# Attention coefficients spread by DMA through DRAM instead of by TensorE, with a new order of first loads, a last tile in two halves and sorted final waits

## The chip, the cores and the metric

The kernel runs on one core of one Trainium2 chip. The metric is device time in microseconds (us) of one execution. Times of single instructions come from one profiled execution of the kernel, taken by the hardware profiler; its own time stands beside the median of the unprofiled runs in the table below.

## The reference

The kernel computes two layers, each made of a linear attention with a learned feature map (A) and a gated feed-forward (B), with residuals around both. The weights are the same in both layers. There are 2048 tokens of width 512, 32 heads of 16, and a hidden width of 1376.

```python
def _A_ref(x, wqkv, w_phi, wo):          # D = 512, H = 32, Dh = 16
    q, k, v = split_heads(x @ wqkv)
    pq = einsum("bhsd,hdf->bhsf", q, w_phi)
    pk = einsum("bhsd,hdf->bhsf", k, w_phi)
    phi_q = concat([softmax(pq), softmax(-pq)], -1)
    phi_k = concat([softmax(pk), softmax(-pk)], -1)
    kv = einsum("bhsf,bhsd->bhfd", phi_k, v)
    z = einsum("bhsf->bhf", phi_k)
    o = einsum("bhqf,bhfd->bhqd", phi_q, kv) / (einsum("bhqf,bhf->bhq", phi_q, z)[..., None] + 1e-6)
    return merge_heads(o) @ wo

def _B_ref(x, W_gate, W_up, W_down):
    return (relu(x @ W_gate) * (x @ W_up)) @ W_down

for layer in range(2):
    x = x + _A_ref(layernorm(x), wqkv, w_phi, wo)
    x = x + _B_ref(layernorm(x), W_gate, W_up, W_down)
```

All tensors are bf16. The kernel folds w_phi into the query and key weights once, at the start (`fold`, giving `Wqp` and `Wkp`).

## The kernel before, in words

**Tiles and slabs.** The 2048 tokens are 16 tiles of 128 tokens (one per partition), and four slabs of four tiles. The code counts slabs from 0 (`st`); the text counts them from 1, so slab 1 is `st` 0. The whole activation stays in SBUF (`x_sb`); DRAM is touched by the loads at the start and by one output DMA for each tile at the end.

**Steps of a slab.** `into_a(st)` makes the layernorm and `keys`: the matmuls of keys and values for each tile, the two exponentials (`expk`, line 484, ScalarE), their sums (`Zk`, VectorE), and `vhat`, the values divided by the sums (line 495, GpSimd), from which TensorE adds up `kvsum`. `sums()` runs once in a layer, after all four slabs: it spreads `kvsum` into the block-diagonal weights `kvbd` and `ZDw`. `out_of_a(st)` makes `queries` (matmuls with `Wqp`, exponentials into `expq`), `attend` and the second layernorm. `glu(st)` makes the feed-forward: 11 chunks of hidden width, each with four matmuls into a gate bank and four into an up bank, ReLU on ScalarE (line 612), the product on VectorE (line 614), then 11 matmuls with `Wd` for each of the four tiles, and the residual (line 597).

**attend.** For each token and head there are two coefficients (one for each sign of the feature map), which divide the unnormalised exponentials by their sums and by the denominator. They are worked out with tokens in the partitions (`atok`, line 561), and TensorE transposes them to `aT`: 64 rows (2 signs x 32 heads) of 512 tokens. `expq` has heads times features in its partitions: eight groups (four chunks `c` by two signs `sg`) of 128 rows, each row set of 16 belonging to one head. So each of 64 rows must be repeated 16 times. The kernel does this by a matmul with the 0/1 matrix `EC`: eight matmuls of 512 columns for a slab, each into a PSUM bank (line 570). For sign 0 VectorE multiplies `expq` by the bank (line 578); for sign 1 (`VIA`) ScalarE first copies the bank to SBUF (`absb`, line 574) and VectorE multiplies by that copy (line 575). Two matmuls with `kvbd` for each chunk then make the numerator (`num`), ScalarE copies it to `oT` (line 583), and four matmuls for each tile with `wo_sb` make the projection. In slab 1 the residual is added by a fifth matmul and copied by ScalarE (line 592), in the others VectorE adds it (line 597).

**The order of the work.** Nothing in the order is written by hand. Every operation is put down with its readers and writers, a cost (`occ`, `lat`) and, for a DMA, a number of bytes; `Program.schedule` then goes through them as a list scheduler: at each step it takes the ready operation with the earliest possible start, and among equal starts the one that was put down first. `plan` sorts by start, gives every engine its fixed instruction order, and works out which semaphores must be waited for. A DMA is priced at 560 ns on its issuing engine, then 630 ns, then its bytes at 270 bytes per ns on one shared queue, then 1170 ns. Every DMA takes the next of 60 semaphores in turn (`N_DSEM`), and at the end `emit` has SyncE (SP) wait for each semaphore that was used, by its number. Loops in the source order are: all four `into_a`, then in each layer `sums`, `out_of_a(0)`, and for each slab `out_of_a(st + 1)`, `glu(st)`, and `into_a(st)` for the next layer or the output DMAs.

**First loads.** On SP: the first tile of x, `wphi`, the second tile of x, `wv`, the rest of x, and the remaining weights. On ScalarE's queue: the key weights in two halves (`ld wk`), ahead of the activation table load.

**Buffers that the change touches.** `expk` and `vhat` have six buffers each (`NE`), `hT` nineteen (`NH`), `absb` three (`NA`).

## Time and profile before

| | |
|---|---|
| Median of 3 runs | 426.74 us (426.41 to 426.89) |
| Profiled execution, its own time | 427.2 us |
| Span of the profiled execution | 425.5 us |
| TensorE (PE) busy | 416.8 us, 98% of the span, 2576 matmuls |
| VectorE (DVE) busy | 278.7 us, 66% |
| ScalarE (ACT) busy | 226.1 us, 53% |
| GpSimd (POOL) busy | 69.2 us, 16% |
| DMA | 10.95 MB in 9598 packets, mean 26 GB/s |

The span runs from the first instruction to the last; the execution's own time has about 1.7 us around it. In the page and the trace's answers, a group of instructions is shown by line, engine, operation and tiles, with busy time and mean duration, and the idle time of the engine before it with what ended that. All matmuls have line 322 (the helper `mm`) and all transposes line 326, so they are told apart by their tiles: `pb<-aT,EC` are the spreading matmuls of `attend`. A matmul's recorded duration is that of a pipelined instruction; the distance from start to start is what it occupies. The page's first part has the busy time of each engine, its second part the span in 40 slices of 10.6 us: VectorE is busy in tenths `7989768984589548883775446887536734863332` of them.

### The profile page before, as it was taken

The numbers are of one execution on the slowest core, as the hardware profiler recorded it, in microseconds if no ns is written. First come the engines' busy times: TensorE is split into PE (matmuls) and PEld (weight loads), VectorE is DVE, ScalarE is ACT, GpSimd is POOL, SyncE is SP. The second block draws the span as 40 slices with busy tenths as digits, with TensorE's granted clock in tenths as the row PEclk, the third lists the DMA queues.
The fourth block names the chain that finished last, engine by engine and source line by source line (L and its number), as shares of the span: only waits on it lengthen the run. The fifth ranks groups of instructions, "written<-read, shape, count | busy, mean of one in ns | idle before, by whom it ended". The sixth has DMA issues, their size and how long they took to land.

```text
span 425.5 us, 6563 instructions
## 1 busy us (share of the span) xinstructions
PE 416.8 (98%) x2576; PEld 209.9 (49%) x2576; DVE 278.7 (66%) x582; ACT 226.1 (53%) x460; POOL 69.2 (16%) x71
## 2 busy tenths in 40 slices
PE   7899999999999999999999999999999999999997
PEld 3455555445445545454455445645444444454443
DVE  7989768984589548883775446887536734863332
ACT  6999888955084514742182169894514522550320
POOL 0439680000008000620043007000000000000000
DMA  8940000000000000000000000000000001000001
GB/s 270 383 144 2 2 0 2 2 1 2 1 2 1 2 0 2 0 2 0 2 0 2 1 2 1 2 2 0 2 25 27 1 0 51 0 2 34 17 0 49
DMA packets 9598, 10.95 MB, mean 26 GB/s; under 512 B 1024, under 2 KB 8544, under 8 KB 9568
## 3 DMA queue, kind: packets, MB, share of 16 engines
q1 hardware_dynamic: 9024, 10.01, 7.0%
q10 hardware_dynamic: 544, 0.52, 0.4%
q8 instruction: 20, 0.33, 0.3%
q14 instruction: 10, 0.08, 0.1%
HBM read 8.44 MB, written 2.10 MB: 25 GB/s over the span
## 4 chain that ended last, share of the span: by engine, by line
PE 88%; ACT 9%; DMA 1%; DVE 0%; SPq 0%; POOL 0%; issue 0%
PE pb L322 85%; PE pb L326 3%; ACT expk L484 3%; ACT ytile L446 2%; DMA wv<-in_A_wqkv_dram 1%; ACT vsb L492 1%; ACT expq L536 1%; ACT Wqp L417 0%; ACT hT L406 0%; ACT yT L460 0%; POOL vhat L495 0%; SPq L345 0%; ACT lnv L435 0%; DVE x_sb L597 0%; DVE atok L561 0%
## 5 line engine op out<-in xcount | busy, mean ns | idle before, releaser
L612 ACT ACTIVATE gate_sb<-pb 128x512 bf16<-128x512 f32 (+1 forms) x88 | 52.7, 598 | 123.3 <-PE pb L322 123.2
L495 POOL TENSOR_TENSOR vhat<-vsb,rZk 128x544 bf16<-128x544 bf16 x64 | 68.4, 1104 | 195.3 <-DVE rZk L488 181.5
L614 DVE TENSOR_TENSOR hT<-gate_sb,pb 128x512 bf16<-128x512 bf16 (+1 forms) x88 | 59.7, 682 | 59.9 <-PE pb L322 59.3
L322 PE MATMUL pb<-yT,Wu 128*128 128x512 bf16 (+1 forms) x352 | 92.8, 379 | 0.0
L322 PE MATMUL pb<-yT,Wg 128*128 128x512 bf16 (+1 forms) x352 | 92.6, 379 | 0.0
L322 PE MATMUL pb<-Wd,hT 128*128 128x512 bf16 (+1 forms) x352 | 77.4, 379 | 0.0
L597 DVE TENSOR_TENSOR x_sb<-x_sb,pb 128x512 bf16<-128x512 bf16 x56 | 36.9, 685 | 46.8 <-PE pb L322 46.7
L322 PEld LDWEIGHTS pb<-Wd,hT 128*128 128x128 bf16 (+1 forms) x352 | 34.4, 98 | 41.5
L322 PEld LDWEIGHTS pb<-yT,Wu 128*128 128x128 bf16 (+1 forms) x352 | 35.1, 100 | 38.5
L322 PEld LDWEIGHTS pb<-yT,Wg 128*128 128x128 bf16 (+1 forms) x352 | 34.6, 100 | 36.8
L486 DVE TENSOR_REDUCE Zk<-expk 128x64 f32<-128x1024 bf16 x32 | 38.4, 1202 | 13.4 <-ACT expk L484 13.3
L432 DVE BATCH_NORM_STATS2 stats<-x_sb 128x6 f32<-128x512 bf16 x64 | 42.5, 676 | 1.9 <-DMA x_sb<-in_A_x_dram 1.1
L536 ACT ACTIVATE expq<-pb 128x512 bf16<-128x512 f32 x64 | 35.3, 703 | 12.8 <-PE pb L322 12.8
L484 ACT ACTIVATE expk<-pb 128x512 bf16<-128x512 f32 x64 | 37.0, 667 | 4.6 <-PE pb L322 3.4
L322 PE MATMUL pb<-wv,yT 128*128 128x512 bf16 x128 | 33.8, 379 | 1.3 <-DMA wv<-in_A_wqkv_dram 1.3
L322 PE MATMUL pb<-wo_sb,oT 128*128 128x512 bf16 x128 | 34.9, 379 | 0.0
L322 PE MATMUL pb<-Wkp,yT 128*128 128x512 bf16 x128 | 33.4, 379 | 1.1 <-ACT yT L460 1.1
L322 PE MATMUL pb<-yT,Wqp 128*128 128x512 bf16 x128 | 32.4, 379 | 0.6 <-ACT Wqp L417 0.5
L574 ACT ACTIVATE absb<-pb 128x512 bf16<-128x512 f32 x32 | 17.8, 623 | 21.3 <-PE pb L322 21.0
L460 ACT ACTIVATE yT<-pb 128x512 bf16<-128x512 bf16 x52 | 27.4, 607 | 2.8 <-PE pb L326 2.7
L322 PE MATMUL pb<-vhat,expk 128*128 128x136 bf16 x256 | 24.3, 223 | 0.1
L322 PEld LDWEIGHTS pb<-vhat,expk 128*128 128x128 bf16 x256 | 18.5, 98 | 10.4 <-POOL vhat L495 1.3
(66 smaller groups left out, 384.5 us busy)
## 6 DMA issues: line engine op xcount, KB each, us to landing
out_dram<-x_sb SPq DMA_DIRECT2D x16, 128.0 KB, 1.7
x_sb<-in_A_x_dram SPq DMA_DIRECT2D x3, 512.0 KB, 9.2
Wg<-in_B_W_gate_dram SPq DMA_DIRECT2D x1, 1376.0 KB, 10.6
Wu<-in_B_W_up_dram SPq DMA_DIRECT2D x1, 1376.0 KB, 12.9
Wd<-in_B_W_down_dram SPq DMA_DIRECT2D x1, 1280.0 KB, 15.8
hT<-in_A_wqkv_dram ACTq DMA_DIRECT2D x2, 256.0 KB, 3.5
wv<-in_A_wqkv_dram SPq DMA_DIRECT2D x1, 512.0 KB, 6.0
hT<-in_A_wqkv_dram SPq DMA_DIRECT2D x1, 512.0 KB, 8.3
```

The costliest lines, as they stand in the source:

```text
L322: op("pe", lambda e: e.matmul(view(ps), lhsT, rhs, start=start, stop=stop), reads=reads, writes=[ps], occ=max(25.0, 0.4167 * n + 2.6), lat ...
L326: op("pe", lambda e: e.transpose(view(ps), src, ident[:]), reads=list(reads) + [R("ident")], writes=[ps], occ=56, lat=220, name=name)
L432: op("dve", (lambda t: lambda e: e.bn_stats(stats[:, t, :], x_sb[:, t, :]))(t), reads=[R("x", t)], writes=[R("st", t)], occ=580, lat=680, ...
L460: op("act", (lambda ps, dst: lambda e: e.activation(dst, b16half(ps).rearrange("p (c n) -> p c n", c=NC), ACT.Copy))(ps, dst), reads=[ps], ...
L484: op("act", (lambda i, s, pk: lambda e: e.activation(expk[:, i, s, :], full(pk), ACT.Exp, scale=1.0 - 2.0 * s))(i, s, pk), reads=[pk], wri ...
L486: op("dve", (lambda i, zb: lambda e: e.tensor_reduce(Zk[:, zb, :], expk[:, i, :, :].rearrange("p s (h f) -> p (s h) f", f=16), AX.X, ALU.a ...
L495: op("pool", (lambda i, s, vb, rz: lambda e: e.tensor_tensor(vhat[:, i, s, :, :], vsb[:, vb, :, :], rZk[:, rz, s * 32:(s + 1) * 32].unsque ...
L536: op("act", (lambda c, s, ps: lambda e: e.activation(expq[:, st, c, s, :], full(ps), ACT.Exp, scale=1.0 - 2.0 * s))(c, s, ps), reads=[ps], ...
L574: op("act", (lambda ab, ps: lambda e: e.activation(absb[:, ab, :], full(ps), ACT.Copy))(ab, ps), reads=[ps], writes=[R("absb", ab)], occ=4 ...
L597: op("dve", lambda e: e.tensor_tensor(x_sb[:, t, :], x_sb[:, t, :], full(ps), ALU.add), reads=[R("x", t), ps], writes=[R("x", t)], occ=597 ...
L612: op("act", (lambda m, gb, pg: lambda e: e.activation(gate_sb[0:m, gb, :], pg.f32()[0:m, :], ACT.Relu))(m, gb, pg), reads=[pg], writes=[R( ...
L614: op("dve", (lambda m, gb, hb, pu: lambda e: e.tensor_tensor(hT[0:m, hb, :], gate_sb[0:m, gb, :], pu.f32()[0:m, :], ALU.mult))(m, gb, hb, pu),
```

## The change

- In slabs 2 to 4 of both layers, `attend` makes no `EC` matmuls. SP stores `aT` (64 rows, 64 KB) to a DRAM tensor (two of them, in turn), waits for that DMA, and issues eight loads; each reads eight rows 16 times over and fills one 128 x 512 tile of `abT` in SBUF. VectorE multiplies `expq` by these tiles. Slab 1 keeps its matmuls, and its ScalarE copies go to `abT`. The columns of `atok` are put in the order of the eight groups.
- `abT` has eight tiles, one for each group, and is shared by all slabs; `absb` goes. `expk` and `vhat` have five buffers instead of six, `hT` eighteen instead of nineteen.
- `wphi` is loaded first on ScalarE's queue, ahead of the key weights, and is priced at 131072 bytes; on SP the second tile of x follows the first.
- The last tile of the last layer is computed in two halves of 256 columns, each with its own eleven matmuls, residual and output DMA; the first half's DMA is issued by ScalarE, the second's by SP.
- At the end SP waits for the DMA semaphores in the order of their last use.

```diff
--- before.py
+++ after.py
@@ -195,6 +195,7 @@
         count = {s: 0 for s in streams}
         known = {e: {s: 0 for s in streams} for e in ENGINES}
         past = {s: {0: {t: 0 for t in streams}} for s in streams}
+        self.last = {}
         self.waits, self.seq = {}, {e: [] for e in ENGINES}
         rr = 0
         for o in order:
@@ -204,6 +205,7 @@
                 assert x.cnt is not None, (o.name, x.name)
                 need[x.stream] = max(need.get(x.stream, 0), x.cnt)
             if o.is_dma:
+                self.last[rr % N_DSEM] = rr
                 o.stream = rr % N_DSEM
                 rr += 1
                 if count[o.stream]:
@@ -239,9 +241,8 @@
             else:
                 ins.then_inc(sems[e], 1)
         if e == "sp":
-            for s in range(N_DSEM):
-                if self.count[s]:
-                    eng.wait_ge(dsems[s], 16 * self.count[s])
+            for s in sorted((s for s in range(N_DSEM) if self.count[s]), key=lambda s: self.last[s]):
+                eng.wait_ge(dsems[s], 16 * self.count[s])
 
 
 def build_kernel(nc, A_x, A_wqkv, A_w_phi, A_wo, W_gate, W_up, W_down, out):
@@ -262,7 +263,7 @@
             return E(nc.sbuf_tensor(name, [P] + list(shape), dt))
 
         NWARM = 8
-        NY, NYT, NE, NV, NG, NH, NA = 4, 6, 6, 4, 3, 19, 3
+        NY, NYT, NE, NV, NG, NH = 4, 6, 5, 4, 3, 18
         x_sb = sb("x_sb", [NT, 512])
         ytile = sb("ytile", [NY, 512])
         yT = sb("yT", [NYT, NC, 512])
@@ -302,7 +303,8 @@
         ident = sb("ident", [128])
         mask8a = sb("mask8a", [8])
         mask8 = sb("mask8", [8])
-        absb = sb("absb", [NA, 512])
+        abT = sb("abT", [8, 512])
+        scratch = [nc.dram_tensor(f"spread{i}", (64, 512), BF16, kind="Internal").ap() for i in range(2)]
         pb = [E(nc.psum_tensor(f"pb{i}", [P, 512], FP32)) for i in range(8)]
 
         made = {}
@@ -346,12 +348,12 @@
                 writes=[R("x", t) for t in range(t0, t1)], nbytes=(t1 - t0) * 131072, name=f"ld x{t0}")
 
         load_x(0, 1)
+        load_x(1, 2)
+        dma("act", lambda e: e.dma_start(wphi[:], A_w_phi.rearrange("(kc hl) d f -> (hl d) kc f", hl=8)),
+            writes=[R("wphi")], nbytes=131072, name="ld wphi")
         for c in (0, 2):
             dma("act", (lambda c: lambda e: e.dma_start(Wknat[:, c:c + 2, :], wqkv_v[:, c:c + 2, 512:1024]))(c),
                 writes=R_Wnat["k"][c:c + 2], nbytes=262144, name="ld wk")
-        dma("sp", lambda e: e.dma_start(wphi[:], A_w_phi.rearrange("(kc hl) d f -> (hl d) kc f", hl=8)),
-            writes=[R("wphi")], nbytes=65536, name="ld wphi")
-        load_x(1, 2)
         dma("sp", lambda e: e.dma_start(wv[:], wqkv_v[:, :, 1024:1536]), writes=[R("wv")], nbytes=524288, name="ld wv")
         load_x(2, 4)
         load_x(4, 8)
@@ -419,8 +421,8 @@
 
         fold("k", Wknat, Wkp)
 
-        cnt = {"y": 0, "yT": 0, "e": 0, "h": 0, "g": 0, "v": 0, "a": 0}
-        VIA = lambda st, c, sg: sg == 1
+        cnt = {"y": 0, "yT": 0, "e": 0, "h": 0, "g": 0, "v": 0, "s": 0}
+        VIA = lambda c, sg: sg == 1
 
         def layernorm(st, step=4, early=False):
 
@@ -558,25 +560,35 @@
             op("act", lambda e: e.activation(zr[:, g], zden[:, g], ACT.Ln), reads=[R("zden", g), R("tables")], writes=[R("zr", g)], occ=200, lat=300, name="zln")
             op("act", lambda e: e.activation(zr[:, g], zr[:, g], ACT.Exp, scale=-1.0), reads=[R("zr", g)], writes=[R("zr", g)], occ=200, lat=300, name="zr")
             for s in range(2):
-                op("dve", (lambda s: lambda e: e.tensor_tensor(atok[:, g, :, s * 32:(s + 1) * 32], Zs[:, g, :, 1 - s, :], zr[:, g], ALU.mult))(s),
+                op("dve", (lambda s: lambda e: e.tensor_tensor(atok[:, g, :, 0:64].rearrange("p t (c s h) -> p t c s h", s=2, h=8)[:, :, :, s, :], Zs[:, g, :, 1 - s, :].rearrange("p t (c h) -> p t c h", h=8),
+                                                               zr[:, g].rearrange("p t (c h) -> p t c h", h=8), ALU.mult))(s),
                    reads=[R("Zs", g), R("zr", g)], writes=[R("atok", g)], occ=195, lat=290, name="atok")
             pa = bank(f"aT{st}")
             for tt in range(4):
                 tr(pa, (lambda tt: lambda p: p.b16()[:, tt * 128:(tt + 1) * 128])(tt), atok[:, g, tt, :], [R("atok", g)], f"aTt{st}")
             op("dve", lambda e: e.tensor_copy(aT[:, g, :], b16half(pa)), reads=[pa], writes=[R("aT", g)], occ=328, lat=415, name="aT")
+            if st:
+                scr = scratch[cnt["s"] % 2]
+                cnt["s"] += 1
+                rs = R("scr", cnt["s"] % 2)
+                dma("sp", lambda e: e.dma_start(scr, aT[0:64, g, :]), reads=[R("aT", g)], writes=[rs], nbytes=65536, name=f"aTo{st}")
+                for gi in range(8):
+                    dma("sp", (lambda gi: lambda e: e.dma_start(abT[:, gi, :], scr[8 * gi:8 * gi + 8, :].unsqueeze(1).to_broadcast([8, 16, 512])))(gi),
+                        reads=[rs], writes=[R("abT", gi)], nbytes=260000, name=f"abT{st}")
             for c in range(NC):
                 for sg in range(2):
-                    ps = bank(f"ab{st}{c}{sg}")
-                    mm(ps, full, EC[:, sg * 4 + c, :], aT[:, g, :], True, True, [R("EC"), R("aT", g)], 512, f"ab{st}")
-                    if VIA(st, c, sg):
-                        ab = cnt["a"] % NA
-                        cnt["a"] += 1
-                        op("act", (lambda ab, ps: lambda e: e.activation(absb[:, ab, :], full(ps), ACT.Copy))(ab, ps), reads=[ps], writes=[R("absb", ab)], occ=480, lat=610, name=f"abc{st}")
-                        op("dve", (lambda c, sg, ab: lambda e: e.tensor_tensor(expq[:, st, c, sg, :], expq[:, st, c, sg, :], absb[:, ab, :], ALU.mult))(c, sg, ab),
-                           reads=[R("eq", st, c, sg), R("absb", ab)], writes=[R("eq", st, c, sg)], occ=335, lat=420, name=f"em{st}", port=True)
-                    else:
+                    gi = 2 * c + sg
+                    if st == 0:
+                        ps = bank(f"ab{st}{c}{sg}")
+                        mm(ps, full, EC[:, gi, :], aT[:, g, :], True, True, [R("EC"), R("aT", g)], 512, f"ab{st}")
+                    if st == 0 and not VIA(c, sg):
                         op("dve", (lambda c, sg, ps: lambda e: e.tensor_tensor(expq[:, st, c, sg, :], expq[:, st, c, sg, :], full(ps), ALU.mult))(c, sg, ps),
-                           reads=[R("eq", st, c, sg), ps], writes=[R("eq", st, c, sg)], occ=595, lat=690, name=f"em{st}")
+                           reads=[R("eq", st, c, sg), ps], writes=[R("eq", st, c, sg)], occ=597, lat=690, name=f"em{st}")
+                        continue
+                    if st == 0:
+                        op("act", (lambda gi, ps: lambda e: e.activation(abT[:, gi, :], full(ps), ACT.Copy))(gi, ps), reads=[ps], writes=[R("abT", gi)], occ=480, lat=610, name=f"abc{st}")
+                    op("dve", (lambda c, sg, gi: lambda e: e.tensor_tensor(expq[:, st, c, sg, :], expq[:, st, c, sg, :], abT[:, gi, :], ALU.mult))(c, sg, gi),
+                       reads=[R("eq", st, c, sg), R("abT", gi)], writes=[R("eq", st, c, sg)], occ=335, lat=425, name=f"em{st}", port=True)
                 pn = bank(f"num{st}{c}")
                 for sg in range(2):
                     mm(pn, full, kvbd[:, sg, c, :], expq[:, st, c, sg, :], sg == 0, sg == 1, [R("kvbd", sg, c), R("eq", st, c, sg)], 512, f"num{st}")
@@ -596,7 +608,7 @@
         def residual(t, ps):
             op("dve", lambda e: e.tensor_tensor(x_sb[:, t, :], x_sb[:, t, :], full(ps), ALU.add), reads=[R("x", t), ps], writes=[R("x", t)], occ=597, lat=690, name=f"res{t}")
 
-        def glu(st, b):
+        def glu(st, b, last=False):
             slots = []
             for fc in range(NF):
                 m = 128 if fc < NF - 1 else FL
@@ -615,12 +627,20 @@
                    reads=[R("gate", gb), pu], writes=[R("hT", hb)], occ=597, lat=690, name=f"h{st}")
             for tt in range(4):
                 t = 4 * st + tt
-                ps = bank(f"d{t}")
-                for fc, hb in enumerate(slots):
-                    m = 128 if fc < NF - 1 else FL
-                    mm(ps, full, hT[0:m, hb, tt * 128:(tt + 1) * 128], Wd[0:m, fc, :], fc == 0, fc == NF - 1,
-                       [R("hT", hb), R("Wd") if fc < NF - 1 else R("WdL")], 512, f"d{t}")
-                residual(t, ps)
+                halves = ((0, 256), (256, 512)) if last and t == NT - 1 else ((0, 512),)
+                for n0, n1 in halves:
+                    ps = bank(f"d{t}")
+                    for fc, hb in enumerate(slots):
+                        m = 128 if fc < NF - 1 else FL
+                        mm(ps, (lambda n: lambda p: p.f32()[:, 0:n])(n1 - n0), hT[0:m, hb, tt * 128:(tt + 1) * 128], Wd[0:m, fc, n0:n1], fc == 0, fc == NF - 1,
+                           [R("hT", hb), R("Wd") if fc < NF - 1 else R("WdL")], n1 - n0, f"d{t}")
+                    if n1 - n0 == 512:
+                        residual(t, ps)
+                    else:
+                        op("dve", (lambda t, n0, n1, ps: lambda e: e.tensor_tensor(x_sb[:, t, n0:n1], x_sb[:, t, n0:n1], ps.f32()[:, 0:n1 - n0], ALU.add))(t, n0, n1, ps),
+                           reads=[R("x", t), ps], writes=[R("xe", n0)], occ=330, lat=420, name=f"res{t}")
+                        dma("sp" if n0 else "act", (lambda t, n0, n1: lambda e: e.dma_start(outv[:, t, n0:n1], x_sb[:, t, n0:n1]))(t, n0, n1),
+                            reads=[R("xe", n0)], writes=[R("out", n0)], nbytes=65536, name=f"out{t}")
 
 
         outv = out.rearrange("b (t p) d -> p (b t) d", p=P)
@@ -644,12 +664,12 @@
             b0 = out_of_a(0)
             for st in range(NS):
                 b1 = out_of_a(st + 1) if st + 1 < NS else None
-                glu(st, b0)
+                glu(st, b0, layer == 1)
                 b0 = b1
                 if layer == 0:
                     into_a(st)
                 else:
-                    for t in range(4 * st, 4 * st + 4):
+                    for t in range(4 * st, min(4 * st + 4, NT - 1)):
                         dma("sp", (lambda t: lambda e: e.dma_start(outv[:, t, :], x_sb[:, t, :]))(t), reads=[R("x", t)], writes=[R("out")], nbytes=131072, name=f"out{t}")
 
         prog.schedule()
```

## The prediction

> **What bounds the kernel now.** I read the chain that ended last, then TensorE's rows in order of time, then the windows by stage.
>
> ```profile
> PE 88%; ACT 9%; DMA 1%; DVE 0%; SPq 0%; POOL 0%; issue 0%
> L322 PE MATMUL pb<-aT,EC 128*128 128x512 bf16 x64 | 17.3, 381 | 0.0
> 88.78 1.03 PE L322 MATMUL pb<-yT,Wu 128*128 128x512 bf16 x4
> 89.64 1.03 PE L322 MATMUL pb<-yT,Wg 128*128 128x512 bf16 x4
> 90.50 1.03 PE L322 MATMUL pb<-yT,Wu 128*128 128x512 bf16 x4
> ```
>
> The chain is TensorE from about 48 to 422.6 us and ScalarE (9%) from 10 to 47. Four matmuls of 512 columns start 0.86 us after the four before them, so one occupies TensorE for 0.2157 us (the 379 ns of a record is a pipelined span, not a price). Nothing is idle between them: what leaves TensorE here leaves the end, if nothing else comes late.
>
> ```profile
> core 0: us, PE busy (x) PEld busy (x) DVE busy (x) ACT busy (x) POOL busy (x), PEclk, DMA share, GB/s
> 71.00:87.00 16.00, 16.00 (x115) 8.04 (x115) 13.81 (x37) 14.96 (x33) 0.00 (x0) 1.00 0.01 2
> 87.00:250.00 163.00, 163.00 (x903) 80.96 (x901) 109.91 (x205) 68.74 (x139) 25.56 (x24) 1.00 0.00 1
> 274.00:291.00 17.00, 16.96 (x121) 8.16 (x120) 13.56 (x37) 15.72 (x34) 0.00 (x0) 1.00 0.00 1
> ```
>
> The windows give busy time by engine. From 87 on VectorE has a third free, ScalarE more, DMA is empty. The two starts of a layer (71 to 87, 274 to 291) are different: all three engines are nearly full, because slab 1's attention and layernorm must be over before the first GLU matmul (87.05 us).
>
> **The matmuls that go.** Six attends (slabs 2 to 4, two layers) lose eight EC matmuls each: 48 x 0.2157 = 10.35 us. VectorE gains too: 24 products move from PSUM to SBUF sources, 676 to 415 ns, 24 x 0.26 = 6.3 us, and ScalarE drops 24 copies (623 ns records, about 0.5 us apart). Neither counts by itself, off the chain.
>
> ```profile
> L578 DVE TENSOR_TENSOR expq<-expq,pb 128x512 bf16<-128x512 bf16 x32 | 21.3, 676 | 0.7 <-PE pb L322 0.7
> L575 DVE TENSOR_TENSOR expq<-expq,absb 128x512 bf16<-128x512 bf16 x32 | 13.0, 415 | 0.0
> L574 ACT ACTIVATE absb<-pb 128x512 bf16<-128x512 f32 x32 | 17.8, 623 | 21.3 <-PE pb L322 21.0 <-DVE mv L433 0.3
> ```
>
> **What replaces them.** One store of aT to DRAM, a wait for it on SP, and eight spreading loads, nine DMAs on SP's queue.
>
> ```profile
> out_dram<-x_sb SPq DMA_DIRECT2D x16, 128.0 KB, 1.7
> 2.26 0.43 SPq L355 DMA_DIRECT2D wv<-in_A_wqkv_dram  x1
> 2.73 1.02 SPq L345 DMA_DIRECT2D x_sb<-in_A_x_dram  x2
> 3.15 0.69 DVE L432 BATCH_NORM_STATS2 stats<-x_sb 128x6 f32<-128x512 bf16 x1 [0.35 <-DMA x_sb<-in_A_x_dram]
> ```
>
> The store costs at most the 1.7 us of an output tile of twice its size. A 128 KB load takes 2.3 us (x's first tile was issued at 0.80, its reader started at 3.15). So the first coefficients are there 1.7 + 0.05 + 2.3 = 4.1 us after the store's issue. Loads follow each other by SP's issue, 0.43 to 0.51 us: the last is there after 7.3 us. No row shows a DMA that reads each row 16 times. From below, the page's peak of 383 GB/s would move 128 KB in 0.34 us, under the issue; from above, SP's issue of 1.42 us for Wg into full queues would make the last 14.0 us. I take about 0.8 us a load, the last after 9.7 us: nearer the short rows, since the queues are empty, with an allowance for the repeated reading. The planner prices a load at 260000 / 270 = 0.96 us and its first at 4.9 us, the last at 11.7, so in the written order VectorE should find coefficients landed when it reaches a product.
>
> The Trainium skill, "DMA: Bandwidth & Descriptors", section "Rules for kernel authors", speaks against these loads: an outermost dimension under 16, here the eight heads, keeps a DMA on at most that many of the 16 engines. No row of before has such a DMA. An estimate by the rule: queue q1's 7.0% of 16 engines' span for 9024 packets is 53 ns a packet, so 128 packets on eight engines take 0.85 us a load and the last lands after 10.0 us instead of 7.3; the sum would be the same for slabs 3 and 4.
>
> What hides those 10 us: for slabs 3 and 4 the GLU of an earlier slab, 132 matmuls or 28.5 us, which TensorE can take first; slab 4 of layer 2 also needs products, projection, residual and layernorm (some 10 us) and still fits. Without that cover 10 us would be paid each time. The loads also stand on SP ahead of output DMAs in layer 2, but these come 2.4 us apart four at a time (first at 314.8 us), and only the last matters.
>
> **Slab 2, at the start of a layer**, has no GLU to hide behind. There its eight EC matmuls were fillers:
>
> ```profile
> 80.43 0.38 PE L322 MATMUL pb<-aT,EC 128*128 128x512 bf16 x1
> 80.86 1.03 PE L322 MATMUL pb<-aT,EC 128*128 128x512 bf16 x4
> 87.05 0.81 PE L322 MATMUL pb<-yT,Wg 128*128 128x512 bf16 x3
> 87.70 1.03 PE L322 MATMUL pb<-wo_sb,oT 128*128 128x512 bf16 x4
> ```
>
> aT of slab 2 is copied at 71.2; its coefficients then land between 75.7 and 81.5. Of slab 1's chain, three products of slab 2 leave VectorE (11 products from 71.55 to 76.8 where slab 1 needs 8: 1.3 us) and three matmuls leave TensorE (0.65 us), so the GLU can start 1 to 1.7 us earlier; num and wo of slab 2 fill from about 78. Bounds: at best the small stalls there now (about 0.5 us a start) vanish as well, -0.5; at worst GLU starts at 85.3 with all 16 wo matmuls of slab 2 left (3.45 us) where now it starts at 87.05 with 4 left (0.86): 88.75 against 87.91 is 0.84 later where 1.73 earlier was counted, +2.6. I take +0.7 a start, 1.4 us in all, near the low end because TensorE has num, wo, transposes and slab 3's and 4's zd matmuls in reach.
>
> **One buffer fewer for expk and vhat** (six to five), and 18 instead of 19 for hT. The tenth tile's exponentials ran at 40.17 us; with five buffers they wait for slab 2's kv matmuls, whose last ten start at 40.89 and end by 41.5. That is up to 1.3 us on ScalarE in the stage it bounds; other applies and copies can be put in front, so 0.3, bounds 0 and 1.3. For hT, eleven of 18 slots belong to one GLU and the next needs its eighth after its first 28 matmul pairs: 0.
>
> **Head.** wphi leaves SP, so x's second tile and wv are issued about 0.47 us earlier; it goes first on ScalarE's queue, so both wk loads, the table load and EC come 0.47 us later. The first exponentials start at 9.91 and need both wv (landed 8.28) and Wkp (copied by 8.24): one comes earlier, one later. Bounds -0.4 and +0.6; I take +0.2, since wk now also meets wv in the queues.
>
> **Tail.** The residual of half a tile: by the rows 571 ns for 408 columns and 429 for 272, 412 ns for 256, against 685: -0.27; 22 matmuls of 256 columns for 11 of 512: +0.03. The final waits:
>
> ```profile
> L244 SPq EVENT_SEMAPHORE  x16: 17/28/28, 423.7 to 425.0; - x16
> SPq L244 <- DMA out_dram<-x_sb: 0.4, 1, 0.4
> ```
>
> 32 DMAs are waited for in 16 records, the first at 423.7; without the 0.4 us spent on the last DMA they run 0.06 us apart and end at 424.6. The change has 16 loads, 54 spreading DMAs and 17 output DMAs, 87 on 60 semaphores: 60 waits, 30 records, 1.8 us from 0.4 us after the last issue, so 2.2 where the landing now ends it at 1.7: +0.45. Putting them in the order of use can't shorten a row of waits already met; it only keeps the last DMA last. Bounds: -0.2 if waits cost nothing and 64 KB lands sooner, +0.5. Tail together -0.27 + 0.03 + 0.45 = +0.2, between -0.5 and +0.3.
>
> **The sum**, for the profiled execution of 427.2 us (span 425.5, 1.7 around it): 427.2 - 10.35 + 1.4 (starts) + 0.3 (expk) + 0.2 (head) + 0.2 (tail) = 418.95. The median of 426.74 lies 0.46 lower: 418.5.
>
> **Rivals.** First, TensorE's saving is paid in full: the DMA is empty and VectorE and ScalarE are relieved at the starts as well, which speaks for it; against it, TensorE needs something to do in those 16 us. 426.74 - 10.35 - 0.5 (stalls) + 0.2 = 416.1. Second, slab 2's coefficients are exposed at both starts: for it speaks that DVE and ACT are at 86% and 93% there, against it that wo can run before the last product. 2 x 2.6 for 2 x 0.7: 418.5 + 3.8 = 422.3. Third, and slower: the spreading loads are slower than the planner's 0.96 us, so VectorE, which runs in its written order, stands before a product with the GLU's hT products (L614) queued behind it, and TensorE stops when its eight PSUM banks are full. The real first landing leads the plan by 0.8 us, and TensorE can run ahead by about 2 us (two or three free banks, each filled in 0.86 us); the saving left is 8.2 / 6 = 1.4 us a slab. So it decides from 0.8 + 2 + 1.4 = 4.2 us over seven loads, that is 0.96 + 0.6 = 1.6 us a load; at 2.0 us a load the lag is 7 x 1.04 - 0.8 = 6.5, less 2, times 6 = 27 us, less 8.2: 445. Against it stand all load rows of this trace, 1.4 us for as much as 512 KB at the page's 383 GB/s. Fourth, the spreading leaves TensorE but the end is set elsewhere, and nothing changes: VectorE's third of free time speaks against it.
>
> **How the numbers follow.** 0.5 for the forecast, 0.24 for the full saving, 0.17 for slab 2 exposed, 0.07 for late loads, 0.02 for no change. A difference under 0.2% (0.85 us) can't be told from none. Faster 0.91, same 0.02, slower 0.07. The range takes in the first two rivals with their unknowns (416.1 less 0.4 for the head; 422.3 and 0.7 of the expk bound): 415.7 to 423.0; the last two, 0.09, and some of the edges lie outside.
>
> **What would show it.** Right: 16 matmuls aT,EC are left; TensorE's busy time falls by about 10 us and stays without gaps from the GLU of slab 1 on; between the last wo of slab 1 and that GLU there are gaps of about a microsecond in each layer; the products of slabs 2 to 4 take 415 ns and idle little before them; loads land 4 to 10 us after the store's issue; 30 records of final waits end about 2.2 us after the last issue. Wrong: VectorE's products waiting for abT by microseconds in slabs 3 and 4 with hT products behind them (third rival), or gaps of over 2 us before the first GLU matmul (second), or first exponentials well after 9.9 us (head).

## The result, and the profile after

The changed kernel takes 422.14 us (median of 4 runs, 421.48 to 423.47), beside 426.81 us (4 runs, 426.41 to 427.12) of the kernel before on the same chip: a ratio of 0.9895, 95% interval 0.9869 to 0.9921, or 4.5 us less where 8.3 us less was forecast. The time lies inside the predicted range and the sign is right, but nearly half of the expected gain is missing. The profiled execution took 421.89 us, its span is 420.2.

The page of the changed kernel: TensorE's row of part 1, the engines' shares of the chain from part 4, and from part 5 the products with coefficients out of SBUF.

```profile
PE 410.0 (98%) x2539; PEld 207.5 (49%) x2539; DVE 272.7 (65%) x583; ACT 214.9 (51%) x436; POOL 69.0 (16%) x71
PE 83%; DVE 7%; ACT 4%; DMA 3%; POOL 1%; issue 1%; SPq 0%; ACTq 0%
L590 DVE TENSOR_TENSOR expq<-expq,abT 128x512 bf16<-128x512 bf16 x56 | 21.9, 418 | 5.7 <-DMA abT<-spread 5.6
```

TensorE still carries the chain, but VectorE has 7% of it (0% before) and DMA 3% (1%): something new stands in TensorE's way. The products take 418 ns as forecast, and the idle time before them is small, 5.7 us over 56. TensorE's busy time fell by 6.8 us, not by the 10.35 that its matmuls occupied: a record of 379 ns is longer than the 216 ns that a matmul occupies, so a matmul that starts 0.1 us late still looks busy. Lateness is therefore measured here from start to start, against the median distance of a matmul's kind (traces of other kernels lack some 2% of the matmul records; such a hole of 0.22 us is not counted). By it the matmuls from the first spreading matmul of layer 1 on were 1.4 us late in all before and are 5.3 us late now, and 10.35 - 3.9 is about the 6.8.

The windows by stage of the changed kernel, with the columns of those shown of before; the last row is the six microseconds in which slab 2's loads run.

```profile
core 0: us, PE busy (x) PEld busy (x) DVE busy (x) ACT busy (x) POOL busy (x), PEclk, DMA share, GB/s
72.00:88.00 16.00, 15.37 (x110) 7.34 (x108) 13.30 (x38) 13.40 (x30) 0.00 (x0) 1.00 0.23 75
272.00:288.00 16.00, 15.45 (x113) 7.62 (x114) 13.35 (x39) 14.17 (x32) 0.00 (x0) 1.00 0.24 79
76.00:82.00 6.00, 6.00 (x52) 3.10 (x53) 4.36 (x14) 5.00 (x11) 0.00 (x0) 1.00 0.51 175
```

TensorE is idle 0.63 and 0.55 us in the two starts, where it was idle 0.00 and 0.04. While the loads run, the 16 DMA engines are busy 0.51 of the time: half of them work. At 175 GB/s a load of 131 KB takes 0.75 us.

The timeline of the changed kernel at the start of layer 1: SP's queue, then VectorE, then TensorE (start, duration, in brackets the idle time before and who ended it).

```profile
72.51 0.53 SPq L574 DMA_DIRECT2D spread<-aT  x1
74.52 5.05 SPq L576 DMA_DIRECT2D abT<-spread  x8
```

```profile
77.32 0.43 DVE L590 TENSOR_TENSOR expq<-expq,abT 128x512 bf16<-128x512 bf16 x1 [0.90 <-DMA abT<-spread]
```

```profile
84.26 0.38 PE L324 MATMUL pb<-expq,kvbd 128*128 128x512 bf16 x1 [0.34 <-DVE ytile L451]
88.31 1.04 PE L324 MATMUL pb<-yT,Wg 128*128 128x512 bf16 x4
```

The store needs 2.0 us, the first product with a loaded tile starts 4.8 us after the store's issue, and the last tile lands at 82.59, 10.1 us after it. VectorE stands 0.9 us for the first tile. From the first spreading matmul to the first GLU matmul it took 16.1 us before (70.96 to 87.05) and takes 16.5 now (71.82 to 88.31); in layer 2 it was 16.3 and is 15.4. Where the prediction let the GLU start 1 to 1.7 us earlier, it starts later in one layer and 0.9 us earlier in the other.

Gaps in slab 4 of both layers were not forecast. In layer 1 TensorE loses 0.9 us there, waiting for GpSimd's `vhat` (from 177.1 us on). In layer 2 it stops twice for a product that waits for its tile; the store before it landed 3.3 us after its issue, where four of the others needed 1.95:

```profile
360.40 0.39 PE L324 MATMUL pb<-expq,kvbd 128*128 128x512 bf16 x1 [0.36 <-DVE expq L590]
362.84 0.39 PE L324 MATMUL pb<-expq,kvbd 128*128 128x512 bf16 x1 [0.32 <-DVE expq L590]
```

The largest surprise is at the head. ScalarE's timeline of the changed kernel, its queue first:

```profile
0.81 0.47 ACTq L352 DMA_DIRECT2D wphi<-in_A_w_phi_dram  x1
1.31 1.04 ACTq L355 DMA_DIRECT2D hT<-in_A_wqkv_dram  x2
8.21 1.08 ACT L408 ACTIVATE hT<-pb 128x512 bf16<-128x512 bf16 x2 [2.35 <-PE pb L328]
13.02 0.60 ACT L486 ACTIVATE expk<-pb 128x512 bf16<-128x512 f32 x1 [0.48 <-PE pb L324]
```

The key weights (`hT` is where they land first) come at 6.21 and 7.73 us, before the change at 4.02 and 4.98; so their transposes are copied at 8.21 (5.34 before) and the first exponentials run at 13.02 instead of 9.91.

### The profile page after: what moved, and what is told of

Same layout as the page of the kernel before. It is cut to its first block, busy times and chain, and to the rows that moved or that the text cites. A ratio compares the mean times of both kernels' runs of the same rounds, so it can differ in the third digit from the quotient of the medians.

```text
span 420.2 us, 6521 instructions
## 1 busy us (share of the span) xinstructions
PE 410.0 (98%) x2539; PEld 207.5 (49%) x2539; DVE 272.7 (65%) x583; ACT 214.9 (51%) x436; POOL 69.0 (16%) x71
## 4 chain that ended last, share of the span: by engine, by line
PE 83%; DVE 7%; ACT 4%; DMA 3%; POOL 1%; issue 1%; SPq 0%; ACTq 0%
PE pb L324 80%; PE pb L328 3%; DVE stats L434 2%; ACT expq L538 2%; DMA hT<-in_A_wqkv_dram 1%; POOL vhat L497 1%; DVE Zk L488 1%; DMA abT<-spread 1%; ACT abT L589 1%; DMA spread<-aT 1%; DVE rZk L490 1%; DVE expq L590 0%; ACT oT L595 0%; DVE mv L435 0%; DVE kvsum L510 0%
## 5 line engine op out<-in xcount | busy, mean ns | idle before, releaser
L324 PE MATMUL pb<-Wd,hT 128*128 128x512 bf16 (+2 forms) x363 | 77.4, 372 | 0.0
L324 PEld LDWEIGHTS pb<-Wd,hT 128*128 128x128 bf16 (+1 forms) x363 | 35.4, 98 | 40.7
L595 ACT ACTIVATE oT<-pb 128x512 bf16<-128x512 f32 x32 | 18.5, 630 | 27.4 <-PE pb L324 27.0
L590 DVE TENSOR_TENSOR expq<-expq,abT 128x512 bf16<-128x512 bf16 x56 | 21.9, 418 | 5.7 <-DMA abT<-spread 5.6
```

Of the source, the lines that this page charges most:

```text
L324: op("pe", lambda e: e.matmul(view(ps), lhsT, rhs, start=start, stop=stop), reads=reads, writes=[ps], occ=max(25.0, 0.4167 * n + 2.6), lat ...
L590: op("dve", (lambda c, sg, gi: lambda e: e.tensor_tensor(expq[:, st, c, sg, :], expq[:, st, c, sg, :], abT[:, gi, :], ALU.mult))(c, sg, gi ...
L595: op("act", (lambda c, pn: lambda e: e.activation(oT[:, g, c, :], full(pn), ACT.Copy))(c, pn), reads=[pn], writes=[R("oT", g, c)], occ=480 ...
```

## The experiments

All times are medians, each with its ratio to the kernel before, measured beside it. To add them up I turn each ratio into microseconds of 426.8; a ratio's interval is worth 0.4 to 1.1 us to either side.

| kernel | time, us | ratio, 95% interval | against before |
|---|---|---|---|
| changed kernel | 422.14 | 0.9895 (0.9869 to 0.9921) | -4.5 |
| e1: changed, old first loads | 419.21 | 0.9821 (0.9807 to 0.9835) | -7.6 |
| e2: before, new first loads | 429.88 | 1.0074 (1.0052 to 1.0095) | +3.2 |
| e3: changed, loads don't wait for the store | 422.01 | 0.9887 (0.9866 to 0.9908) | -4.8 |
| e4: changed, slab 2 by matmuls | 421.73 | 0.9875 (0.9855 to 0.9894) | -5.3 |
| f1: e1, slab 2 by matmuls | 421.04 | 0.9860 (0.9846 to 0.9874) | -6.0 |
| f2: e1, only slab 2 by DMA | 425.98 | 0.9979 (0.9969 to 0.9988) | -0.9 |
| f3: e1, loads don't wait for the store | 419.68 | 0.9824 (0.9810 to 0.9837) | -7.5 |
| f4: changed, wphi behind the key weights | 424.36 | 0.9939 (0.9915 to 0.9962) | -2.6 |
| g1: before, fewer buffers | 427.93 | 1.0022 (1.0013 to 1.0031) | +0.9 |
| g2: e1, loads priced lower | 421.88 | 0.9886 (0.9868 to 0.9904) | -4.9 |
| g3: e1, sixteen source rows, few final waits | 418.65 | 0.9800 (0.9786 to 0.9814) | -8.5 |
| h3: e1, a second wphi on ScalarE's queue | 419.07 | 0.9816 (0.9802 to 0.9830) | -7.9 |

**e1: the old first loads in the changed kernel.**

```diff
-        load_x(1, 2)
-        dma("act", ... wphi ..., nbytes=131072)
         for c in (0, 2):
             dma("act", ... Wknat ...)
+        dma("sp", ... wphi ..., nbytes=65536)
+        load_x(1, 2)
         dma("sp", ... wv ...)
```

> The changed kernel with the first loads in their old order (wphi second on SP, key weights first on ScalarE's queue). In the changed kernel the second half of the key weights landed at 7.73 us instead of 4.98, and slab 1's first EC matmul came at 71.8 us instead of 71.0. Theory (the order of loads costs the 0.9 us): first EC matmul back at about 71.0, time 422.1 - 0.9 = 421.2 us. Rival (the sixth buffer of expk and vhat costs it): the key weights land at 5 us again, but the first EC matmul stays at 71.8 and the time at 422.1.

ScalarE's timeline of this kernel, with the same rows as above:

```profile
0.81 0.99 ACTq L352 DMA_DIRECT2D hT<-in_A_wqkv_dram  x2
5.90 1.13 ACT L408 ACTIVATE hT<-pb 128x512 bf16<-128x512 bf16 x2 [1.21 <-PE pb L328]
9.85 1.08 ACT L486 ACTIVATE expk<-pb 128x512 bf16<-128x512 f32 x2
```

The keys land at 3.8 and 5.0 us, the first exponentials run at 9.85, and the kernel gains 7.6 us. The new first loads take 3.2 us of the gain away. In the two traces the difference lies ahead of layer 1's first spreading matmul (69.69 us here, 71.82 in the changed kernel); from there to the end they agree within 0.1 us. The order that the scheduler wrote for the head is another one, too.

**e2: the new first loads alone**, in the kernel before (the same lines the other way round).

> The kernel before with the new order of the first loads and nothing else. Theory: key weights' second half lands at about 7.7 us, first EC matmul about 0.9 us later than 70.96, time 426.8 + 0.9 = 427.7 us. Rival (buffers): first EC matmul at 71.0, 426.8 us.

The other side of the same term: +3.2 us, with no other line changed. The two expectations had the loads right and their price, 0.9 us, too low. The keys landed at 5.03 and 7.00 us, the first exponentials ran at 11.15. The profiled execution took 427.91 us, 2 us less than the median, so the trace shows only a part: in it the first GLU matmul starts at 87.17 us (87.05 before), and the span is 0.7 us longer than before.

**e3: loads that don't wait for the store**, to see what the way through DRAM costs. They read rows of `wo` from DRAM, so the coefficients are other numbers; the store stays.

```diff
-                    dma("sp", ... abT[:, gi, :] <- scr[8 * gi:8 * gi + 8, :] ..., reads=[rs])
+                    dma("sp", ... abT[:, gi, :] <- A_wo[8 * gi:8 * gi + 8, :] ...)
```

> The changed kernel whose spreading loads read the first 64 rows of the output projection's weights instead of the stored coefficients, so that they don't wait for the store and can be issued long before; the coefficients of slabs 2 to 4 are wrong. Number and size of all DMAs stay. Theory (the way through DRAM comes too late for slab 2, 2.4 us in both layers, and for slab 4, 1.9 us): TensorE's gaps before the first GLU and in slab 4 go, 422.1 - 4.3 = 417.8 us. Rival (the gaps come from the planner's new order or from the extra traffic, not from lateness): 421.5 to 422.5 us.

Nothing that can be told from the changed kernel: -4.8 against -4.5 us, and the intervals overlap.

The traces of the changed kernel, e3 and e4 (below) show more of the head. The three have the same first loads and, up to 59 us, the same order on ScalarE, VectorE and GpSimd. Yet the first exponentials run at 13.02, 11.30 and 14.58 us, and the first matmul with `ZDw` starts at 64.56, 62.85 and 66.13: what is late at the first exponentials is as late there. The sixteen matmuls that fold `wphi` into the keys, in TensorE's timeline of the changed kernel, of e3 and of e4:

```profile
9.46 1.58 PE L324 MATMUL pb<-hT 128*128 128x128 bf16 x16
```

```profile
8.17 1.11 PE L324 MATMUL pb<-hT 128*128 128x128 bf16 x16
```

```profile
9.58 1.91 PE L324 MATMUL pb<-hT 128*128 128x128 bf16 x16
```

The same instructions start 107 ns apart in e4, 56 ns apart in e3 but for two short waits, and in the changed kernel change from the one to the other at 10.5 us. The clock records of the traces begin with the full granted clock at 10.54 us (changed kernel), 6.12 (e3) and 13.61 (e4). From the start of the transposes of the second half of the keys (7.77, 7.20 and 7.90 us) to the first exponentials it takes 5.3, 4.1 and 6.7 us. So 1.2 us of the changed kernel's lateness against e3, and 2.6 of e4's, lie in TensorE's pace and not in the landing of the keys.

**e4: slab 2 by matmuls again**, slabs 3 and 4 by DMA.

```diff
-            if st:
+            if not (st < 2):
                 scr = scratch[cnt["s"] % 2]
...
-                    if st == 0:
+                    if st < 2:
                         ps = bank(f"ab{st}{c}{sg}")
```

> The changed kernel with EC matmuls in slabs 1 and 2, spreading DMAs in slabs 3 and 4 alone: 16 matmuls (3.45 us) more on TensorE. Theory (slab 2's late coefficients cost 2.4 us in the two layers): 422.1 + 3.45 - 2.4 = 423.2 us, with the gaps before the first GLU back to those of before. Rival (slab 2 was paid in full and the loss lies elsewhere): 422.1 + 3.45 = 425.6 us.

With eight matmuls more in each layer the time is the same (-5.3 against -4.5, overlapping), below both expectations. The gaps in slab 4 are gone, and what TensorE is late at the starts is 0.71 and 0.75 us instead of 1.75 and 1.50. With the new first loads slab 2's DMA brings nothing that can be told.

After these four my theory was: the head costs 3 us, and slab 2's coefficients come too late through DRAM. The next kernels all have the old first loads, so that the head is out of the way.

**f1: e1 with slab 2 by matmuls** (the edits of e1 and e4).

> The changed kernel with the first loads in their old order, EC matmuls in slabs 1 and 2, spreading DMAs in slabs 3 and 4: 16 matmuls (3.45 us) more on TensorE than with old loads alone (419.2 us). Theory (slab 2's saved matmuls are given back as gaps at the starts of the layers and as a gap in slab 4): 419.2 us, from first EC matmul of a layer to the next 200.0 and 144.3 us. Rival (slab 2's DMA is worth its 3.45 us): 422.7 us.

-6.0 us, between the two expectations. Slabs 3 and 4 alone should give 32 x 0.2157 = 6.9, less the price of the smaller buffers (0.9, below) and 0.1 for the tail: 5.9. Within the interval of 0.6 they are paid in full.

**f2: only slab 2 by DMA**, slabs 3 and 4 by matmuls.

```diff
-            if st:
+            if st == 1:
...
-                    if st == 0:
+                    if st != 1:
```

> The changed kernel, its first loads in their old order, with spreading DMAs in slab 2 alone (EC matmuls in slabs 1, 3 and 4): 16 matmuls less than before. Theory (slab 2's saving is not paid): first EC matmul of layer 1 to that of layer 2 203.0 to 203.6 us against 203.48 before, layer 2 147.3 to 147.9 against 147.74; time 425.5 to 426.8 us, as far as the startup is that of before. Rival (it is paid): 1.7 us less in each layer, 423.3 us.

-0.9 us: of 3.45 us of matmuls and with 0.9 + 0.1 paid for buffers and tail, 3.45 - 1.0 - 0.9 = 1.5 us are lost. From f1 to e1 the same step brings 1.7 of 3.45. So slab 2 costs 1.5 to 1.8 us over both layers (with 0.6 to 0.9 either way), where the prediction had 1.4.

**f3: e1 with loads that don't wait for the store** (the edits of e1 and e3).

> The changed kernel with old order of loads, whose spreading loads read 64 rows of the output projection's weights and so wait for no store; the coefficients of slabs 2 to 4 are wrong. Theory (lateness of the way through DRAM is what leaves slab 2 unpaid): 3.5 us under the 419.2 of the same kernel with the wait, 415.7 us. Rival (the start of a layer is bound by the chain of VectorE and ScalarE up to the first GLU matmul, whatever slab 2 does): 418 to 419 us.

-7.5 against -7.6 us: my theory fell, and 419.68 us is above the rival's 419 as well. The tiles are there, as the waits show, first of e1, then of f3 (microseconds in total, times, longest):

```profile
DVE expq L590 <- DMA abT<-spread: 4.9, 7, 1.3
```

```profile
DVE expq L590 <- DMA abT<-in_A_wo_dram: 1.4, 2, 1.1
```

Yet the matmuls of the starts are late by 2.29 and 1.00 us (e1: 1.56 and 1.54). Only the gap in slab 4 of layer 2 is gone (0.03 against 1.07 us). So at the starts it is not the coefficients alone that are short. The reading left is that other work is: VectorE and ScalarE must bring slab 1 to the GLU, and TensorE has lost its fillers. This is argued, not shown, since the scheduler wrote another order for f3.

**f4: wphi behind the key weights on ScalarE's queue**, the rest of the new order kept.

```diff
         load_x(1, 2)
-        dma("act", ... wphi ...)
         for c in (0, 2):
             dma("act", ... Wknat ...)
+        dma("act", ... wphi ...)
```

> The changed kernel with one move in its first loads: wphi stays on ScalarE's queue but behind the two halves of the key weights, and SP keeps the new order, with wv issued at 1.7 us. Theory (the key weights are late because they are issued half a microsecond later and then share the engines with wv): key weights land at about 5 us and the time is 419 us, as with the old order. Rival (it is wv's earlier issue alone): key weights land after 6 us and the time is over 421 us.

A miss: slower than the changed kernel, 424.36 us. The keys land at 4.06 and 5.25, as in the old order, but now `wphi` is the late one (issued at 1.83, landed at 7.19), and the folding needs both; the first exponentials run at 10.91. They are earlier than in the changed kernel and yet the time is longer. In its trace TensorE has the full clock from 5.12 us on, but by the seventeenth of the `expk` exponentials ScalarE is 3.7 us behind e1 (41.14 us against 37.44), having taken `expq` earlier (22.76 against 25.93), and the first start of a layer is late by 3.27 us. So a part lies in the order that the scheduler wrote for this variant. The profiled execution was 1.8 us faster than the median; that rest stays open.

**g1: fewer buffers alone** (five of `expk` and `vhat`, eighteen of `hT`) in the kernel before.

```diff
-        NY, NYT, NE, NV, NG, NH, NA = 4, 6, 6, 4, 3, 19, 3
+        NY, NYT, NE, NV, NG, NH, NA = 4, 6, 5, 4, 3, 18, 3
```

> The kernel before with five buffers for expk and vhat and 18 for hT, nothing else. Theory (the buffer that is missing costs next to nothing, and moves only the planner's order): 426.4 to 427.4 us, within 0.3 of before. Rival (it costs up to 1.3 us in the startup): first EC matmul after 71.5 us and 427.7 us or more.

+0.9 us (0.6 to 1.3), where 0.3 was taken. It is not where I put it, behind the tenth tile's exponentials: the first spreading matmul even starts 1.06 us earlier (69.90). It is paid in the first start, TensorE's timeline of g1:

```profile
81.58 0.39 PE L322 MATMUL pb<-wo_sb,oT 128*128 128x512 bf16 x1 [0.38 <-ACT absb L574]
85.83 0.40 PE L326 MATMUL pb<-ident,ytile 128*128 128x128 bf16 x4 [0.27 <-DVE aT L566]
87.57 0.59 PE L322 MATMUL pb<-yT,Wg 128*128 128x512 bf16 x2
```

With fewer buffers the scheduler writes another order; TensorE is late by 2.30 us in this start (0.50 before), and the first GLU matmul starts at 87.57 instead of 87.05. f1 shows the same gaps, 0.38, 0.18, 0.21 and 0.27 us, in the same places. Which of the two buffers does it was not tried.

**g2: the spreading loads priced at 0.72 us instead of 0.96** in e1, near the 0.75 us measured.

```diff
-                        reads=[rs], writes=[R("abT", gi)], nbytes=260000, name=f"abT{st}")
+                        reads=[rs], writes=[R("abT", gi)], nbytes=195000, name=f"abT{st}")
```

> The changed kernel with the old order of loads, the planner's price of a spreading load cut from 0.96 to 0.72 us, which is what the loads took in the trace. Only the written order changes. Theory (the gaps at the starts are those of a chain, which the order of slab 2's products hardly touches): 419.2 us within 0.7, gaps at the two starts 1.5 us each as before. Rival (the order written for late coefficients makes the gaps): gaps under 0.8 us at each start, 417.7 us or less.

2.7 us slower than e1. The two starts together are as long as e1's (from the first spreading to the first GLU matmul 16.28 and 15.85 us, e1 16.65 and 15.42); from layer 1's first GLU matmul to layer 2's it takes 201.4 us instead of 199.4. The third rival in small: the plan puts products earlier, and VectorE and TensorE stand in their order. VectorE, then TensorE, of this kernel in slab 4 of layer 2:

```profile
360.19 0.42 DVE L590 TENSOR_TENSOR expq<-expq,abT 128x512 bf16<-128x512 bf16 x1 [2.08 <-DMA abT<-spread]
```

```profile
360.67 0.39 PE L324 MATMUL pb<-expq,kvbd 128*128 128x512 bf16 x1 [1.56 <-DVE expq L590]
```

The higher price is no error of the plan but its margin.

**g3: sixteen source rows and few final waits** in e1. The store writes every row twice, and each load reads sixteen rows eight times; at the end SP waits only for DMAs that it has not already waited for.

```diff
-        scratch = ... (64, 512) ...
+        scratch = ... (64, 2, 512) ...
-  dma("sp", scr <- aT[0:64, g, :])
+  dma("sp", scr <- aT[0:64, g, :].unsqueeze(1).to_broadcast([64, 2, 512]))
-  abT[:, gi, :] <- scr[8 * gi:8 * gi + 8, :].unsqueeze(1).to_broadcast([8, 16, 512])
+  abT[:, gi, :] <- scr[8 * gi:8 * gi + 8].rearrange("h d n -> (h d) n").unsqueeze(1).to_broadcast([16, 8, 512])
-  for s in sorted((s for s in range(N_DSEM) if self.count[s]), ...)
+  for s in sorted((s for s in range(N_DSEM) if self.count[s] > self.known["sp"][s]), ...)
```

> The changed kernel with the old order of loads and two edits whose effects lie in different places. The store writes each row of aT twice, so that a spreading load has 16 source rows in its outermost dimension instead of eight; and SP waits at the end only for DMAs whose end it doesn't know yet through other waits. Theory: DMA share during the loads rises towards 1 in bursts and a load's packets take 0.4 instead of 0.7 us, but SP's issue of 0.62 us a load bounds them then, so nothing is gained before the last matmul; from the last matmul's start to the end of the span 2.9 us instead of 3.37, since the 30 records of waits go. Time 419.2 - 0.5 = 418.7 us. Rival (late coefficients are what costs): about 1 us less up to the last matmul as well, 417.7 us.

The fastest version: 418.65 us, 2.0% under the kernel before (1.9 to 2.1). The final waits of the changed kernel and of g3 (how many, their duration in ns, first and last start):

```profile
L245 SPq EVENT_SEMAPHORE  x30: 17/28/28, 417.9 to 419.7; - x30
```

```profile
L245 SPq EVENT_SEMAPHORE  x1: 28/28/28, 416.4 to 416.4; - x1
```

From the last matmul's start to the end it is 2.76 us instead of 3.37: 0.6 us for 29 waits. The loads gain little. Their window in g3:

```profile
74.00:80.00 6.00, 6.00 (x53) 3.15 (x52) 3.84 (x11) 4.83 (x11) 0.00 (x0) 1.00 0.56 173
```

A DMA share of 0.56 for 0.51, and 173 GB/s where it was 175. A load's semaphore now counts sixteen engines' landings, where it counted eight, but SP issues the loads 0.56 to 0.65 us apart, once after 1.56 (eight in 5.97 us). The engines are idle for nearly half of the time, so the issue is now the limit. The order on ScalarE and VectorE is that of e1; the gap in slab 4 of layer 2 is gone (0.04 us), but layer 1 is 0.5 us longer than in e1. The intervals of e1 and g3 touch, so the two halves of this edit are not told apart by the times.

**h3: a second wphi first on ScalarE's queue** in e1, to find which part of the new order makes the keys late. SP's queue stays old.

```diff
+        dma("act", ... abT[:, 0, 0:64] <- A_w_phi ..., nbytes=131072)
         for c in (0, 2):
             dma("act", ... Wknat ...)
```

> The changed kernel with the old order of first loads (e1_old_loads), and a second copy of wphi (16 KB, into a tile that is not used before the first attend) issued first on ScalarE's queue, ahead of the key weights. SyncE's queue is as in the kernel before: wphi second, wv at 2.3 us. So the key weights are issued half a microsecond later, behind 512 packets of 32 bytes, as in the changed kernel, but wv and the second tile of x are not earlier. Theory A (the keys come late because wv, issued half a microsecond earlier on SyncE's queue, shares the 16 DMA engines with them): the keys land at about 4.5 and 5.5 us instead of 6.2 and 7.7, the first exponentials run by 10.6 us instead of 13.0, and the time is at most 1 us over e1_old_loads' 419.2, so 419.2 to 420.2. Theory B (the small packets and the later place in ScalarE's own queue are the cause): the keys land at 6 to 7.7, the first exponentials run after 11.5, and the time is that of the changed kernel, 421.5 to 422.5. Between 420.2 and 421.5 both have a share.

ScalarE's timeline of h3:

```profile
1.31 1.05 ACTq L354 DMA_DIRECT2D hT<-in_A_wqkv_dram  x2
10.16 1.08 ACT L488 ACTIVATE expk<-pb 128x512 bf16<-128x512 f32 x2 [0.65 <-PE pb L324]
```

The keys are issued as late as in the changed kernel and behind as many small packets, and land at 5.27 and 6.28 us (6.21 and 7.73 there, 3.84 and 4.99 in e1); the first exponentials run at 10.16, and the time is that of e1: about theory A's time, though the keys land 0.8 us after its 4.5 and 5.5. So the place on ScalarE's queue alone costs nothing that can be measured. The other half of the new order is SP's queue: the second tile of x and `wv` (512 KB) are issued 0.5 us earlier, `wv` ahead of the second half of the keys. f4 has that without the later place, and its keys land at 4.06 and 5.25. Only both moves together bring the keys as late as in the changed kernel. The times of these variants carry their written order as well: h3 starts its first GLU matmul 1.8 us before e1 (84.57 and 86.35) and loses that again in layer 1.

## Why the prediction was right and wrong

**The step that failed: the head.** It was taken at +0.2 us, with bounds of -0.4 and +0.6. Four pairs of kernels differ in the first loads alone: the new ones cost 3.2 us from before to e2, 3.2 from e1 to the changed kernel, 2.7 from f3 to e3 and 0.7 from f1 to e4, each with about 1 us either way. The prediction shifted the landings by the 0.47 us of the issue and held that one of the two inputs of the first exponentials came earlier and one later; "wk now also meets wv in the queues" was in it, without a price. The runs show two things in its place.

The first is the meeting. In the changed kernel the keys came 2.2 and 2.75 us later, `wv` only 0.36 us earlier (8.28 to 7.92). The later place alone (h3) and the earlier `wv` alone (f4) each leave the keys at 6.28 us or before. Both bounds were made of issue times; a bound from bytes (`wv` is as large as both halves of the keys) would have been several times wider.

The second is TensorE's clock, which the prediction did not have. With the old first loads TensorE has its full clock by 7.5 us at the latest in all nine traces, and `wv` (8.0 us in e1) is awaited anyway. With the new ones the full clock came at 5.1 to 13.6 us; in the changed kernel, e2, e3 and e4 TensorE stands idle from 4.9 us until the keys land, and the folding comes after that. In e3, where it came at 6.12, the first matmul with `ZDw` starts only 0.3 us later than in e1 (62.85 and 62.51), near the 0.2 forecast; in the changed kernel, where it came at 10.54, it is 2.1 us later, and in e4 3.6. The three profiled executions with the full clock by 6.2 us (e2, e3, f4) were each 1.8 to 2.1 us faster than their kernel's median. This suggests that the other executions had it later, but their clocks are not on record. So how the 3.2 us divides between the landing of the keys, the clock and the written order is open, and so is why the pair of f1 and e4 shows 0.7.

That the time lies in the range is luck: its upper end was made for slab 2 exposed, not for the head.

**The matmuls that go** were right. Slabs 3 and 4 are paid in full (f1), and the sum of terms measured in other kernels closes for e1: -10.35 + 1.5 (slab 2, f2) + 0.9 (buffers, g1) + 0.1 (tail) = -7.85, measured -7.6. (Slab 2's 1.5 was found by taking off the 0.9 and the 0.1, so what this tests is that f2's -0.9 and the 6.9 of slabs 3 and 4 add up.) With 3.2 for the head (e2) it is -4.65, where the result is -4.5. The products in 418 ns, the 48 loads, the cover by the GLU of an earlier slab and the 16 matmuls left are as written.

**The starts**: 1.4 us was taken, 1.5 to 1.8 measured, but not by the route described. In the changed kernel's trace TensorE is later than before by 1.25 and 0.75 us at the starts (g1 has 1.8 at the first by its buffers alone), and by 0.9 and 1.0 us in slab 4 of the two layers, which the prediction had at nothing ("still fits"): 3.9 us. e1, with the same gaps within 0.2 us, gets 1.3 us back ahead of its first spreading matmul (69.69 us, before 70.96), which with 0.1 for the tail leaves the 2.7 us that it lacks of 10.35. The GLU did not start 1 to 1.7 us earlier in layer 1. In layer 2 the gap in slab 4 is lateness of the tiles, since it goes in g3, where they come earlier in the same written order. In layer 1, where TensorE waits for GpSimd's `vhat`, it stays in g3 and h3; e3 and f3, in another written order, don't have it. With slab 2 by matmuls neither shows, and why was not tried.

**The loads**: forecast 4.1 us from the store's issue to the first tile and 9.7 to the last at 0.8 us a load; measured 4.8, 10.1 and 0.75. The store, taken at 1.7 us at most, needed 1.95 (3.3 once). The Trainium skill, "DMA: Bandwidth & Descriptors", section "Rules for kernel authors", holds that eight rows in the outermost dimension keep a DMA on at most eight of the 16 engines. This trace agrees: a DMA share of 0.51 while the loads run, and eight engines' landings counted for each load. The prediction's estimate of 0.85 us a load by this rule was near the measured 0.75.

**The term for the buffers** was too small: 0.3 taken, 0.9 measured, inside the bounds of 0 and 1.3, but by another order at the first start rather than by waiting exponentials. **The tail** was right: 30 wait records that end 2.1 us after the last issue at 417.56 (2.2 forecast), and 3.37 us from the last matmul's start to the end where it was 3.29.

**The rivals.** The full saving (416.1) is not reached by any kernel here; g3 comes to 418.65. Slab 2 exposed (422.3) has the right time by accident: its mechanism is worth 0.1 to 0.4 us more than the forecast, and the 422.14 comes from the head. The late loads (445) have a real mechanism, which g2 shows in small with a lower price; with the price as it is, loads of 0.75 us stay under the plan's 0.96.

## What to carry to other kernels

When loads at the start of a kernel change places, ask for each which bytes it now shares the DMA engines with, and look at what TensorE does meanwhile and at which clock it then runs: half a microsecond of issue order became 3 us in the medians here, but only 0.3 us ahead of the first matmul with `ZDw` in e3's trace, where TensorE was early at its full clock. One profiled execution does not stand for all where the times spread by 4 us. Work taken from the engine that sets the end is paid in full only where that engine has other work in reach, so split such a change by stage, and keep the old way where the removed work was a filler. In an order that is planned ahead, a price above the measured duration can be margin: cutting it to the measured value cost 2.7 us here.

## What the runs showed of the hardware that was not expected

- TensorE's full clock came at 4.3 to 7.5 us in the nine traces with the old first loads and at 5.1 to 13.6 in the five with the new ones. Until then matmuls of 128 columns start 107 ns apart, after it 56.
- The first loads' order changes the spread of the times. The five kernels with the new order spread by 2.0 to 4.2 us over 4 to 7 runs (changed kernel 421.48 to 423.47, f4 422.54 to 426.77), those with the old order by 0.5 to 2.3 over 4 to 12 (h3 418.74 to 419.28, f2 425.56 to 427.90).
- A spreading load occupies SP's queue for about 0.62 us (eight in 5.05), a plain load 0.43 to 0.51. With sixteen source rows the issue, not the DMA engines, sets the pace.
- A store of 64 KB to DRAM took 1.95 us to its landing, longer than the 1.7 us of an output tile of 128 KB.
- A load of 512 packets of 32 bytes ahead of the key weights in the same queue, which also put their issue off by 0.5 us, went with a landing 1.3 to 1.4 us later in the trace of h3 than in that of e1, and cost no measurable time (419.07 against 419.21 us).
